# Tail scores of a cosine attention as two 64-row, 64-column products instead of one zero-padded full product, with a new order of the work

## The chip, the core and the metric

The kernel runs on one core of one Trainium2 chip. A core has a matrix engine (PE, whose weight loads are listed apart as PEld), a vector engine (DVE), an activation engine (ACT), a general engine (POOL) and a queue engine (SP), each with its own in-order list of instructions. The metric is the device time of one execution in microseconds (us); the median of several runs is compared.

## What is computed

Cosine attention over 8 batches, 12 heads, 448 tokens and a head size of 64, and then one highway layer over 3584 tokens of width 768:

```python
q_n = q / (np.linalg.norm(q, axis=-1, keepdims=True) + 1e-06)
k_n = k / (np.linalg.norm(k, axis=-1, keepdims=True) + 1e-06)
scores = np.matmul(q_n, k_n.transpose(0, 1, 3, 2)) / tau
attn = softmax(scores)                      # over the last axis
attn_out = np.matmul(attn, v)
x = attn_out.transpose(0, 2, 1, 3).reshape(B * S, H * D)
H = np.maximum(x @ w_h, 0.0)
T = 1.0 / (1.0 + np.exp(-(x @ w_t + b_t)))
out = T * H + (1.0 - T) * x
```

## The kernel before

The work is done batch by batch (`b`), and inside a batch by pairs of heads (`p`): head `p` and head `p + 6` share one tile of 128 partitions, 64 for each, because the head size is 64. For each batch the kernel squares and sums q and k (ACT and DVE), takes inverse roots by two Newton steps on DVE (L416 to L423, seven small instructions), scales q and k (`qn` L434, `kp` L495, `kb` L502, mostly on POOL), turns them with PE transposes (L446, L460, L465) and copies the results back with DVE (`qT` L451, `kT` L471 to L475).

The 448 keys of a head are three chunks of 128 and a tail of 64. `scores` (from L524) makes, for each pair of heads:

- for each of the three chunks two products of 64 rows by 128 columns (L531), one for each head. The one reads partitions 0 to 63 and the other 64 to 127, and each writes a PSUM tile `B` of its own;
- for the tails of both heads one product of 128 rows by 128 columns (L542). Columns 384 to 511 of `kT` come from `kb`, in which rows 0 to 63 are filled for the first head's columns alone and rows 64 to 127 for the second head's; the rest was set to zero at the start (L266). So one full product gives both heads' tail scores in one tile, 64 partitions each;
- an exponential on ACT for each of the seven tiles (L537 into `E`, L544 into `Et`).

`attend` (from L548) multiplies the exponentials with v: full products of 128 by 128 (L556 from `Et`, L561 from `E`) and, for the last 64 queries, products of 128 rows by 64 columns, two of which stand side by side in one tile (L569). DVE divides by the sums (L576, L577). The layer (`ffn`, from L583) turns x (L600), multiplies it with `wt` and `wh` (L616, or in two halves of 64 columns L613 for the last rows of a batch), and DVE, ACT and POOL make the gate and the output (L625 to L642), which SP stores (L649, L652).

So PE works with matmuls of three shapes: 128 by 128 (letter F in the code), 64 by 128 (letter T: L531) and 128 by 64 (letter C: L569 and L613). The letter is the `mode` given to each operation. Nothing that runs reads it: it belongs to the search that wrote the order.

All operations are listed first (1915 of them, from the loop at L656), and `ORDER` (L18) is a written-out permutation of them. It sets the order of instructions on every engine and of the loads and stores on every queue. `SLOTS` (L97) says which buffer of its ring each tile takes; `B` has eight PSUM buffers. Semaphores between engines follow from the order and the buffers. `PORT` adds a wait of some POOL operations on a DVE operation before them in the order.

At the start 18 products of zeros (L279) keep PE busy while the first q and k arrive.

Of the kernel before, what the change touches and what calls it, by code (L numbers as in the profile page):

```python
# [95 lines left out]

SLOTS = {  # L97
    "qr": "01010101",
    "kr": "0120120",
    "kt": "01010101",  # L100
    "kb": "01010101",
    "kp": "012345012345012345012345012345021435021435120534",
    "vr": "01010101",
    "vt": "01011010",
    "vp": "01010101",
    "sq": "0120120102102102102102012012022102102102102021020",
    "n2": "01010101",
    "y": "01201201",
# [661 lines left out]
```

## Time and profile before

| | |
|---|---|
| median of three runs | 271.36 us (271.6, 271.36, 269.6) |
| the profiled execution's own time | 270.06 us |
| its span from first to last instruction | 268.3 us |
| mean granted PE clock | 0.958 |
| PE busy | 251.6 us (94%), 3042 matmuls |
| DVE busy | 233.4 us (87%) |
| ACT busy | 214.5 us (80%) |
| POOL busy | 169.8 us (63%) |

A row of a group of instructions reads: line, engine, operation, tile written and tile read, shape (for a matmul rows\*columns of the array, then the moving operand), count, and then busy time in us, mean duration of one in ns, and the idle time just before them with what ended it. A row of the timeline starts with the start in us from the span's start and the duration of the merged instructions. A matmul's duration reaches to its modelled end, long after the next one has begun; what a matmul costs PE is the distance from its start to the next start.

### The profile page before, as it was taken

Reading aid. Unit: us, or ns where it says so; the run is one execution under the profiler, and the core shown is the slowest. Engines: PE = TensorE matmul, PEld = TensorE weight load, DVE = VectorE, ACT = ScalarE, POOL = GpSimd, SP = SyncE. Lnnn points to the kernel's source line nnn. Section 1 sums busy time; section 2 is a strip of 40 time slices with the busy share of each in tenths; the row PEclk is TensorE's granted clock in tenths of the full one; section 3 lists DMA queues with packets and bytes.
Section 4 is the critical chain, followed back from the end, with each engine's and each line's share of the span. In section 5 each row is a group of like instructions: output and inputs, shape, how many; then the busy total and the mean of one; then the engine's idle time right before and its main releaser. Section 6 shows DMA issues by size and latency. Waiting matters only on the chain.

```text
span 268.3 us, 7687 instructions
## 1 busy us (share of the span) xinstructions
PE 251.6 (94%) x3042; PEld 158.8 (59%) x3042; DVE 233.4 (87%) x523; ACT 214.5 (80%) x421; POOL 169.8 (63%) x212
## 2 busy tenths in 40 slices
PE   8375999999999999999999999999999999999990
PEld 2122566656756576657656685666666675667660
DVE  2987988799999999999989899999998788657993
ACT  3389899999589997999899996999979757883120
POOL 6467878306975679668957397659555686320650
PEclk9755799999999999999999999999999999999998
DMA  7999999999307990496995972990513101052146
GB/s 173 298 290 181 208 270 261 213 255 126 44 18 221 234 182 14 146 257 159 151 142 185 164 107 67 330 135 4 147 23 100 29 15 49 0 147 65 29 135 190
DMA packets 51092, 38.64 MB, mean 144 GB/s; under 512 B 37488, under 2 KB 47856, under 8 KB 51056
## 3 DMA queue, kind: packets, MB, share of 16 engines
q1 hardware_dynamic: 25888, 26.75, 36.2%
q0 software_dynamic: 24896, 11.21, 33.1%
q8 instruction: 24, 0.39, 0.5%
q10 hardware_dynamic: 272, 0.20, 0.2%
q14 instruction: 12, 0.10, 0.1%
HBM read 38.34 MB, written 11.01 MB: 184 GB/s over the span
## 4 chain that ended last, share of the span: by engine, by line
PE 81%; DMA 6%; DVE 4%; ACT 4%; SPq 1%; issue 1%; POOL 1%; ACTq 0%; DVEq 0%
PE B L616 33%; PE B L531 12%; PE B L561 10%; PE B L613 5%; DMA os<-in_k_dram 4%; PE B L556 4%; PE B L600 4%; PE B L446 3%; PE B L542 3%; PE B L569 3%; PE B L460 3%; ACT E L537 3%; DMA out_dram<-os 1%; PE B L465 1%; DVE hm L628 1%
## 5 line engine op out<-in xcount | busy, mean ns | idle before, releaser
L537 ACT ACTIVATE E<-B 128x448 f16<-128x448 f32 x288 | 137.4, 577 | 15.6 <-PE B L531 12.6
L642 POOL TENSOR_TENSOR os<-x,hm 128x384 f32<-128x384 f16 x53 | 47.5, 911 | 50.2 <-DVE hm L637 39.6
L616 PEld LDWEIGHTS <-xT 128*128 128x128 f16 x576 | 51.2, 98 | 34.8 <-issue 7.5
L434 POOL TENSOR_TENSOR qn<-qr,y 128x448 f16<-128x448 f32 x47 | 43.4, 934 | 24.6 <-issue 8.1
L616 PE MATMUL B<-wh,xT 128*128 128x384 f16 x288 | 57.6, 326 | 0.0
L616 PE MATMUL B<-wt,xT 128*128 128x384 f16 x288 | 56.7, 326 | 0.0
L531 PE MATMUL B<-qT,kT 64*128 64x448 f16 x288 | 43.5, 367 | 2.8 <-DVE kT L473 1.5
L561 PE MATMUL B<-vp,E 128*128 128x65 f16 x864 | 44.5, 195 | 0.0
L561 PEld LDWEIGHTS <-E 128*128 128x128 f16 x864 | 39.1, 99 | 2.9
L632 ACT ACTIVATE tt<-z 128x768 f16<-128x768 f32 (+1 forms) x32 | 25.3, 793 | 18.5 <-DVE z L625 14.8
L495 POOL TENSOR_TENSOR kp<-kr,y 128x384 f16<-128x384 f16 x42 | 34.3, 827 | 8.2 <-DVE tt L634 2.6
L628 DVE SCALAR_TENSOR_TENSOR hm<-B,x 128x384 f16<-128x384 f32 x56 | 30.5, 549 | 3.0 <-PE B L616 1.7
L556 PE MATMUL B<-vp,Et 128*128 128x130 f16 x144 | 32.3, 224 | 0.0
L625 DVE TENSOR_TENSOR z<-B,bias 128x384 f32<-128x384 f32 x48 | 25.9, 551 | 6.5 <-PE B L616 5.5
L544 ACT ACTIVATE Et<-B 128x448 f16<-128x448 f32 x48 | 27.9, 597 | 3.1 <-PE B L542 2.8
L577 DVE SCALAR_TENSOR_TENSOR x<-B,rd 128x448 f16<-128x448 f32 x48 | 29.2, 617 | 0.6
L376 DVE TENSOR_REDUCE n<-sq 128x14 f32<-128x896 f32 (+1 forms) x25 | 25.8, 1040 | 1.2 <-ACT sq L368 1.2
L397 DVE TENSOR_REDUCE n<-sq 128x18 f32<-128x1152 f32 (+2 forms) x17 | 21.5, 1269 | 4.2 <-ACT sq L388 3.8
L368 ACT ACTIVATE sq<-qr 128x896 f32<-128x896 f32 (+1 forms) x24 | 23.1, 978 | 1.1 <-DMA qr<-in_q_dram 1.1
L531 PEld LDWEIGHTS <-kT 64*128 64x128 f16 x288 | 10.3, 94 | 20.1 <-issue 12.3
L556 PEld LDWEIGHTS <-Et 128*128 128x128 f16 x144 | 14.1, 98 | 7.9 <-issue 4.7
L542 PE MATMUL B<-qT,kT 128*128 128x448 f16 x48 | 17.4, 371 | 1.1 <-DVE kT L475 1.1
(59 smaller groups left out, 363.3 us busy)
## 6 DMA issues: line engine op xcount, KB each, us to landing
qr<-in_q_dram SPq DMA_DIRECT2D x7, 1344.0 KB, 7.6
out_dram<-os SPq DMA_DIRECT2D x48, 192.0 KB, 3.3
kr<-in_k_dram POOLq DMA_DIRECT2D x7, 576.0 KB, 12.2
vr<-in_v_dram POOLq DMA_DIRECT2D x7, 576.0 KB, 10.3
kt<-in_k_dram SPq DMA_DIRECT2D x16, 96.0 KB, 6.4
vt<-in_v_dram SPq DMA_DIRECT2D x16, 96.0 KB, 7.5
out_dram<-os SPq DMA_DIRECT2D x16, 96.0 KB, 2.9
qr<-in_q_dram SPq DMA_DIRECT2D x3, 448.0 KB, 6.9
```

Of the source, the lines that this page charges most:

```text
L434: ENG[eng].tensor_mul(R("qn", 3 * b + g)[:, :, t, :], R("qr", b)[:, g + 3 * t, :].rearrange("l (j d) -> l j d", d=D), R("y", b)[:, c : c + ...
L495: ENG[eng].tensor_mul(R("kp", 6 * b + p).rearrange("l c t d -> l t c d"), a, kcol(b, p))
L531: nc.tensor.matmul(R("B", ("S", n, c, t))[:, 0:S], lhsT=R("kT", i)[ln, s, 128 * c : 128 * c + 128], rhs=R("qT", i)[ln, s, :], start=True, ...
L537: nc.scalar.activation(R("E", n)[:, at : at + 7, :].rearrange("l j x -> l (j x)"), R("B", ("S", n, c, t))[:, 0:S], AF.Exp)
L544: op("ACT", f"expt {n}", lambda: nc.scalar.activation(R("Et", n).rearrange("l j x -> l (j x)"), R("B", ("St", n))[:, 0:S], AF.Exp), r=[("B ...
L556: nc.tensor.matmul(U[:, 2 * c : 2 * c + 2, :], lhsT=Et[:, 2 * c : 2 * c + 2, :].rearrange("l j x -> l (j x)"), rhs=vp[:, 6:8, 0:65], start ...
L561: nc.tensor.matmul(U[:, 2 * c + t, :], lhsT=E[:, at : at + 2, :].rearrange("l j x -> l (j x)"), rhs=vp[:, 3 * t + m, 0:65], start=False, s ...
L577: op("DVE", f"ev {n}", lambda: nc.vector.scalar_tensor_tensor(out=R("x", b)[:, :, D * p : D * p + D], in0=U_()[:, :, 0:D], scalar=0.0, in1 ...
L616: nc.tensor.matmul(P[:, 0:MH], lhsT=xT[:, cc, :], rhs=w_[:, cc, MH * mh : MH * mh + MH], start=(cc == 0), stop=(cc == CC - 1))
L625: op("DVE", f"za {g} {mh}", lambda at=at, sl=sl: nc.vector.tensor_add(R("z", g)[:, sl], R("B", at)[:, 0:MH], biast[:, :] if tail else bias ...
L628: op("DVE", f"hm {g} {mh}", lambda at=at, sl=sl, mh=mh: nc.vector.scalar_tensor_tensor(out=R("hm", g)[:, sl], in0=R("B", at)[:, 0:MH], sca ...
L642: op(eng, f"out {g} {mh}", lambda sl=sl, mh=mh: ENG[eng].tensor_add(R("os", g)[:, sl], xpart(mh), R("hm", g)[:, sl]), r=[("gg", g), ("x", ...
```

## The change

The full tail product becomes two products of 64 rows by 64 columns. The first reads partitions 0 to 63 of `kT` and `qT` and writes partitions 0 to 63 of the tile; the second does the same with partitions 64 to 127. Both write the same PSUM tile. The exponential after them, the zeros in `kb` and the transposes stay. PE gets 48 matmuls and 48 weight loads more. The operation's letter goes from F to T. `ORDER` and `SLOTS` are replaced throughout, so every engine and every queue has a new order of the same operations. Lines after L543 move by three: the tail products are L544 and their exponential L547 in the changed kernel.

```diff
 ORDER = tuple(
     int(n)
     for n in """
-6 26 41 25 5 43 4 42 16 24 27 14 1 2 29 45 28 44 54 46 47 56 35 48 49 50 51 55 52 8 53 33 3 34 37 94 306 36 0 308 12
...
-1891 1897 1898 1906 1909 1900 1910 1907 1899 1672 1908 1911 1912 1913 1901 1914
+1 26 25 6 5 35 24 29 9 4 23 28 8 11 27 7 3 16 18 19 30 12 17 2 33 14 45 43 20 41 10 34 46 21 44 22 32 13 42 15 31 56
...
+1904 1897 1905 1898 1909 1906 1861 1910 1899 1907 1900 1908 1901 1911 1912 1913 1914
 """.split()
 )
...
-    "kp": "012345012345012345012345012345021435021435120534",
+    "kp": "012345012354012345012435012345012345130245130245",
...
         def ft():
-            nc.tensor.matmul(R("B", ("St", n))[:, 0:S], lhsT=R("kT", i)[:, s, 384:512], rhs=R("qT", i)[:, s, :], start=True, stop=True)
-        op("PE", f"qkt {n}", ft, r=[("qT", i, s), ("kT", i, "t")], w=[("B", ("St", n))], mode="F")
+            for t in range(2):
+                ln = slice(64 * t, 64 * t + 64)
+                nc.tensor.matmul(R("B", ("St", n))[ln, 0:S], lhsT=R("kT", i)[ln, s, 384 + 64 * t : 448 + 64 * t],
+                                 rhs=R("qT", i)[ln, s, :], start=True, stop=True)
+        op("PE", f"qkt {n}", ft, r=[("qT", i, s), ("kT", i, "t")], w=[("B", ("St", n))], mode="T")
```

What the new order moves can be read from the built programs. On PE, most of the 48 tail products stood between full products before; now 13 pairs stand inside a run of L531, and all others but one at an end of such a run. At the start, POOL issues the first two loads of v ahead of the zeroing of `vp` (before: between its two halves); SP issues the first tails of k after two more of the first loads of k, and the first tails of v after all first loads of q and k; DVE has both copies of the first values (L509) ahead of the last step of the first Newton iteration (before: the first of them ran at 19.5 us), and the first `kT` copy ahead of the second half of the first `qT` copy. The last 24 products of PE and everything after them stand as before, with other buffers.

More of the change, by code (lines that the diff above doesn't have):

```diff
@@ L101 @@
     "kb": "01010101",
-    "kp": "012345012345012345012345012345021435021435120534",
+    "kp": "012345012354012345012435012345012345130245130245",
     "vr": "01010101",
-    "vt": "01011010",
+    "vt": "01010101",
     "vp": "01010101",
-    "sq": "0120120102102102102102012012022102102102102021020",
+    "sq": "0120120120122102012012012102100120212011012021120",
     "n2": "01010101",
     "y": "01201201",
-    "tu": "010101010101",
-    "qn": "012012012012012012021021",
+    "tu": "010110101010",
@@ L111 @@
+    "qn": "012012012021021012012102",
     "qT": "012012012012012012012012",
     "kT": "012012012012012012012012",
-    "E": "012012012100210211021021021201201021021201210202",
-    "Et": "012010210122102011201201201121021211021021210210",
-    "rd": "010101010101010101010101010101010101010101010100",
+    "E": "012012012011210120210212021201201201201201102202",
+    "Et": "012012102100201020210210201201021021021021012012",
+    "rd": "010101010110101010100101011010101010101010101010",
     "x": "01201201",
-    "xT": "01220120120121021021021201200210",
@@ L118 @@
-    "z": "01011010100101010101010101011010",
-    "tt": "01100101011010010100101001001010",
-    "hm": "01201021201202102102012101020120",
-    "os": "01230120230210323012021302131230201",
-    "B": (
-        "0123456701234567012345670124761462074357410523714501204503216402564731206471035246357243170463514267"
-        "0352416105246310724625713604236175467137632576013425617305340621743074602510243715623015621435604605"
-        "3176453102645367524103675214074316425137542613026301426541275104304157350175240671425042034215047165"
-        "4027365412751620516243546273150423156027435067132740631647210635740625317023465023167402315401637542"
-        "6540216427031265473627051346203637512016745321734527014630612745312745613042631541257631405732461567"
-        "4302175235701645031756243501623741056423104276510623641725107456301725370316745302614753014672"
+    "xT": "01201201201202102102102012011201",
@@ new lines @@
+    "z": "01011011010101010101011010101010",
+    "tt": "01010101101010101010101001010101",
+    "hm": "01201012120102102102012201201021",
+    "os": "01230123012020130130310231023120321",
+    "B": (
+        "0123456701234567012345670124015672305167346230472046232561470234265710247132054670542630746135270512"
+        "7302641376525074630215734602173405252402302716405231674251765310742631053612746572103572315047560324"
+        "1057361542610356407123560742106754320175462037461256073075361743157602436571032754106210476513426734"
+        "1263514073604175306706254673267031245763410236541726543071043527614032576041567034215607135204312765"
+        "0364523670247160352473641053264051430214250361740126543702415067342640715635746302136231075431620576"
+        "1453021570312654215346721354201572634016532041573215604237152043157604361570231754236051273461"
```

142 rows, old and new, of the table ORDER are left out of this document.

## The prediction

> **What bounds the kernel now.** I read the page first: the busy shares, the slices, and the chain that ended last.
>
> ```profile
> span 268.3 us, 7687 instructions
> PE 251.6 (94%) x3042; PEld 158.8 (59%) x3042; DVE 233.4 (87%) x523; ACT 214.5 (80%) x421; POOL 169.8 (63%) x212
> ...
> PE   8375999999999999999999999999999999999990
> ...
> PEclk9755799999999999999999999999999999999998
> ...
> PE 81%; DMA 6%; DVE 4%; ACT 4%; SPq 1%; issue 1%; POOL 1%; ACTq 0%; DVEq 0%
> ```
>
> PE makes up 81% of the chain, and from the sixth slice on (about 34 us) it is full in every slice but the last. A full PE row alone proves little, because a matmul's end is modelled. So I took the groups of PE with their idle time in the first 35 us, and the busy time by stretch.
>
> ```profile
> L531 PE MATMUL B<-qT,kT 64*128 64x448 f16 x26 | 7.5, 497 | 2.7 <-DVE kT L473 1.5 <-DVE qT L451 0.7 <-ACT E L537 0.3
> L279 PE MATMUL B<-wz 128*128 128x512 f16 x18 | 6.8, 559 | 1.3 <-DVE wz L266 1.3
> ...
> L446 PE MATMUL B<-ident,qn 128*128 128x128 f16 x21 | 2.4, 280 | 4.1 <-DVE tu L421 4.1
> ...
> L542 PE MATMUL B<-qT,kT 128*128 128x448 f16 x4 | 2.0, 560 | 1.1 <-DVE kT L475 1.1
> L465 PE MATMUL B<-ident,kb 128*128 128x128 f16 x6 | 1.2, 298 | 1.0 <-DVE kT L473 1.0
> ```
>
> ```profile
> 34.40:262.00 227.60, 227.33 (x2878) 147.53 (x2875) 205.88 (x443) 191.00 (x377) 145.74 (x173) 1.00 0.63 130
> ```
>
> All that PE waited for others lies in the first 35 us (4.1 + 2.7 + 1.1 + 1.0, and 1.3 before the first product of zeros). Between 36 and 262 us the list of PE's waits is empty: of 227.60 us it is busy for 227.33. So from about 34 us to the end of the last product the time is the sum of PE's issue distances: a tenth of a microsecond more or less on PE is a tenth in the result, and there is no wait that could swallow it.
>
> **The change part by part: the products.** What a matmul costs PE is the distance of starts, which the timeline shows to 0.01 us.
>
> ```profile
> 101.19 0.50 PE L600 MATMUL B<-ident,x 128*128 128x128 f16 x6
> 101.52 0.55 PE L446 MATMUL B<-ident,qn 128*128 128x128 f16 x7
> ...
> 102.89 0.50 PE L600 MATMUL B<-ident,x 128*128 128x128 f16 x6
> 103.32 0.74 PE L531 MATMUL B<-qT,kT 64*128 64x448 f16 x6
> 103.99 1.15 PE L616 MATMUL B<-wt,xT 128*128 128x384 f16 x6
> 104.98 0.35 PE L542 MATMUL B<-qT,kT 128*128 128x448 f16 x1
> 105.17 1.14 PE L616 MATMUL B<-wt,xT 128*128 128x384 f16 x6
> 106.24 0.55 PE L531 MATMUL B<-qT,kT 64*128 64x448 f16 x4
> 106.72 0.51 PE L460 MATMUL B<-ident,kp 128*128 128x128 f16 x6
> ...
> 110.48 0.28 PE L569 MATMUL B<-vp,E 128*64 128x65 f16 x6
> 110.61 0.20 PE L569 MATMUL B<-vp,Et 128*64 128x65 f16 x2
> 110.73 0.23 PE L556 MATMUL B<-vp,Et 128*128 128x130 f16 x1
> ```
>
> The full tail product takes 0.19 us (104.98 to 105.17). Six L531 take 0.67 us and four take 0.48, so one pair of 64-row products costs 0.19 us too: the two run beside each other. A pair of 64 by 64 products that overlap in the same way streams the same 448 columns, so it costs 0.19 us as well. The zero rows of the full product never cost time; streaming gains nothing (48 x 0.00 us). The nearest weight load to the 48 new ones:
>
> ```profile
> L569 PEld LDWEIGHTS <-E 128*64 128x64 f16 x288 | 8.1, 111 | 6.7 <-issue 5.1 <-ACT E L537 0.5
> ```
>
> Uncovered they would cost 48 x 0.111 = 5.3 us. But the six L569 above, each with such a load, issue within 0.13 us: the loads hide under the products. I cost them at 0.
>
> **The switches between shapes.** The same rows show what it costs to change the shape. Six L616 take 0.99 us before a full product and 1.07 before an L531 (+0.08). Six transposes take 0.33 before full ones and 0.43 before an L531 (+0.10). Leaving L531 costs 0.67 - 3 x 0.19 = 0.10. For shapes that differ in columns alone I took another window.
>
> ```profile
> 98.63 0.35 PE L561 MATMUL B<-vp,E 128*128 128x65 f16 x6
> 98.81 0.22 PE L556 MATMUL B<-vp,Et 128*128 128x130 f16 x1
> 98.88 0.35 PE L561 MATMUL B<-vp,E 128*128 128x65 f16 x6
> 99.16 0.28 PE L569 MATMUL B<-vp,E 128*64 128x65 f16 x6
> 99.28 0.20 PE L569 MATMUL B<-vp,Et 128*64 128x65 f16 x2
> 99.31 0.98 PE L613 MATMUL B<-wh,xT 128*64 128x384 f16 x10
> ```
>
> Six L561 take 0.18 us before another full product and 0.28 before an L569 (+0.10); two L569 take 0.03 before an L613 of the same shape (99.28 to 99.31), and 0.12 before a full product (110.61 to 110.73, +0.09). So every change of shape costs (0.08 + 0.10 + 0.10 + 0.10 + 0.09) / 5 = 0.094 us, whether rows or columns differ; where the shape stays, as from L569 to L613, nothing is paid.
>
> I then walked PE's list of both built programs and counted changes of shape. Before there are 176. After there are 222 if 64 by 64 is a shape of its own: 55 of them are between a tail pair and an L531. There are 167 if it counts as the same as L531, as the letter T assumes. What a change between 64 by 128 and 64 by 64 costs, no row of before shows. The bounds are 0 us (as between L569 and L613) and 0.10 us. I take 0.094: the nearest row is 128 by 128 to 128 by 64, where rows are equal and columns differ as here, and it pays in full in both directions. That is 46 x 0.094 = +4.3 us. With 0 it is -9 x 0.094 = -0.85 us.
>
> The Trainium skill, page "TensorEngine Tiling (Array Packing)", section "Tiling Modes", lists 64x64 and 64x128 as two configurations and says that changing the mode, not just the tile, drains the engine. By that rule the sum stays +4.3 us, and the letter T would have been the wrong label; the trace agrees for the three shapes that it shows, and no row here has the fourth.
>
> **The start.** The new order also changes the first 34 us, in which PE waits for others. On DVE, two value copies now stand inside the first Newton iteration.
>
> ```profile
> 6.12 0.55 DVE L397 TENSOR_REDUCE n<-sq 128x6 f32<-128x384 f32 x1 [3.83 <-ACT sq L388]
> ...
> 9.92 0.18 DVE L423 SCALAR_TENSOR_TENSOR y<-tu,y 128x20 f32<-128x20 f32 x1
> 10.01 0.94 DVE L397 TENSOR_REDUCE n<-sq 128x12 f32<-128x768 f32 x1
> ...
> 11.34 0.62 DVE L434 TENSOR_TENSOR qn<-qr,y 128x448 f16<-128x448 f32 x1
> ...
> 14.42 0.35 DVE L473 COPY kT<-B 128x384 f16<-128x384 f16 x1
> ...
> 15.65 1.72 POOL L502 TENSOR_TENSOR kb<-kt,y 64x384 f16<-64x384 f32 x2
> ...
> 19.54 0.45 DVE L509 COPY vp<-vr 128x576 f16<-128x576 f16 x1
> ```
>
> ```profile
> vr<-in_v_dram POOLq DMA_DIRECT2D x2, 144.0 KB, 6.6
> ```
>
> The two copies (2 x 0.45) and the reduction (0.94), which comes forward too, would end the iteration 1.8 us later. Against that, the reductions of q no longer wait behind that of k (0.55 us), and the first `qn` of DVE, which ran at 11.34 us behind the 0.94 us reduction, does not have it ahead any more; the first transposes on PE need both halves, so they hardly move. The first `kT` copy, at 14.42 us the last thing before the first L531, comes forward by one `qT` half and one `kp`, 0.9 us in all. On SP the first tails of k now go behind two loads of k, and their square and sum come later too; `kb`, which needs the sum, ran only at 15.65 us on POOL, which covers that. So a gain of up to 0.9 us is one end. The other: the copies wait for the first loads of v, which land 6.6 us after issue; they are issued a microsecond or so earlier than before, at some 1.3 us, and land near 8 and 9 us, in time. If they take 2.5 us more, DVE and all behind it (`qn`, `kp`, the `qT` copy, then PE) are late by that: +2.5 us. I take 0, since the two named effects nearly cancel and the loads are near to in time.
>
> The steady order is new as well, on every queue. PE had no wait there and becomes slower, so DVE (205.88 of 227.60 us), ACT and POOL get more room: I cost it at 0, covered by PE; should one load or ring be late, its price is that wait. The loads and stores stay the same in number and size. The end (last gate, output, store) is the same sequence: 0.
>
> **The sum.** 268.3 + 4.3 + 0 = 272.6 us of span; the execution's own time is 270.06, 1.8 above its span, so 274.4. The median of the three runs, 271.36, is 1.3 us above this execution and one run (269.6) is below it. I set the forecast between: the mean of the four executions is 270.7, plus 4.3 gives 275.0 us.
>
> **Rivals.** First, on the other side: 64 by 64 is the same mode as 64 by 128 and no change is paid inside a run of L531. The sum is then -0.85 us: 269.8 us. It speaks for it that the row halves are the same; against it, that a change of columns alone is paid between L561 and L569. The point of decision: with 55 changes at x each, the total is -0.85 + 55x, so it is not slower from x below 0.015 us. Second, the two products do not overlap. Each pair then costs 2 x 0.19, and 48 x 0.19 = 9.1 us come on top: 284.1 us. For it speaks that the two L531 of a pair write two PSUM tiles, while these write one; against it, that the pairs of L569 write halves of one tile and overlap (two in 0.03 us). The same page's section "Restrictions and Gotchas" says that different row tiles cannot use one PSUM bank at a time, which would be this rival; no row here has two row halves in one bank. Third, the new start wins more than I see, by 2 to 3 us of the 8.9 that PE waits for q and k there: 272.5 us.
>
> **How the numbers follow.** Forecast 0.67, with its own range 273.2 to 277.6 us (start -0.9 to +2.5, and some for the spread of runs); no change paid 0.15; no overlap 0.08; a shorter start 0.10. A measurement of this kernel can tell about 1% from no change, here 268.6 to 274.1 us. Slower by over 1%: 0.58 of the forecast's 0.67, and 0.08, together 0.66. Within: 0.09 + 0.10 + 0.11 = 0.30. Faster: the rest of the first rival, with a shorter start, 0.04. The range from 269.4 to 277.6 us takes in the first and third rivals and leaves out the second and tails.
>
> **What would show it.** In the changed trace's timeline, the product before a tail pair inside a run of L531 shows 0.29 us to the next start, not 0.19, and again on the way back; a single pair takes 0.19 us plus that. If the way there and back costs nothing, the first rival holds; if the two starts of a pair are 0.19 us apart, the second. PE's waits should again end near 34 us; a later first row of L569, or waits on ACT, DVE or DMA after 40 us, would show that the new order, not the shape, moved the time. I am wrong above all if the fourth shape is not its own mode.

## The result, and the profile after

The changed kernel takes 273.12 us (median of 9 runs, 272.1 to 274.77). The kernel before took 269.74 us beside it (9 runs, 269.17 to 271.6). The ratio is 1.0112, with a 95% interval of 1.0081 to 1.0144: slower by 2.2 to 3.9 us, in the middle 3.0; the two medians lie 3.4 apart. The forecast was 275.0 us, from a base of 270.7 and a loss of 4.3. The direction held, and so did the range over the rivals, 269.4 to 277.6 us. The forecast's own range, 273.2 to 277.6, was missed by 0.1 us: the result lies just below it. Of the 1.9 us between forecast and median, 1.0 is the base (269.74 is the better measured one) and 0.9 is the loss itself.

These lines of the page after answer to those shown of before: span and busy times, PE's and the clock's slices, the chain by engine.

```profile
span 271.1 us, 7813 instructions
...
PE 254.8 (94%) x3090; PEld 157.6 (58%) x3090; DVE 231.7 (85%) x523; ACT 214.9 (79%) x421; POOL 170.1 (63%) x212
...
PE   8278899999999999999999999999999999999990
...
PEclk9757999999999999999999999999999999999998
...
PE 85%; DVE 6%; issue 3%; ACT 2%; DMA 1%; SPq 1%; POOL 1%; DVEq 0%
```

PE's fourth slice is fuller than before (8 for 5) and its clock there higher (7 for 5), and PE has more of the chain (85% for 81%); yet the span is 2.8 us longer, 271.1 for 268.3. The busy times by stretch (PE, PEld, DVE, ACT, POOL, then granted clock, DMA share, GB/s) show where nothing is lost:

```profile
0.00:34.40 34.40, 24.54 (x192) 12.01 (x193) 27.36 (x80) 25.54 (x48) 24.43 (x40) 0.80 1.17 242
34.40:265.00 230.60, 230.23 (x2900) 145.61 (x2898) 202.23 (x440) 189.25 (x374) 145.66 (x173) 1.00 0.63 126
```

From 34.4 us on PE is busy for 230.23 of 230.60 us, and the list of its waits is again empty from 36 us on. So the new time is not a wait. PE's waits of the whole execution (releaser, then us in total, times, longest) all lie in the start:

```profile
PE B L446 <- POOL qn L434: 5.2, 1, 5.2
PE B L279 <- DVE wz L266: 1.3, 1, 1.3
PE B L531 <- DVE kT L473: 1.2, 2, 0.8
PE B L559 <- ACT Et L547: 0.5, 1, 0.5
PE B L531 <- ACT Et L547: 0.5, 1, 0.5
```

With four more of 0.2 us they make 9.5 us, before about 10.0. The place that the prediction named is in the timeline of PE:

```profile
38.53 0.35 PE L564 MATMUL B<-vp,E 128*128 128x65 f16 x6
38.81 0.38 PE L544 MATMUL B<-qT,kT 64*64 64x448 f16 x2
39.12 0.36 PE L531 MATMUL B<-qT,kT 64*128 64x448 f16 x2
39.41 0.38 PE L544 MATMUL B<-qT,kT 64*64 64x448 f16 x2
39.72 0.36 PE L531 MATMUL B<-qT,kT 64*128 64x448 f16 x2
```

Read the distances of starts. Six L564 take 0.28 us before a tail pair (0.18 with no change behind them). The L531 pair between two tail pairs takes 0.29, where two such products take 0.19: the way into 64 by 64 costs 0.10. The tail pairs take 0.31: 0.12 more than the 0.19 of a full product with no change behind it. So 64 by 64 is a shape of its own, and both ways are paid.

### The profile page after: what moved, and what is told of

Read it like the earlier page. It is cut to its first block, busy times and chain, and to the rows that moved or that the text cites. A ratio compares the mean times of both kernels' runs of the same rounds, so it can differ in the third digit from the quotient of the medians.

```text
span 271.1 us, 7813 instructions
## 1 busy us (share of the span) xinstructions
PE 254.8 (94%) x3090; PEld 157.6 (58%) x3090; DVE 231.7 (85%) x523; ACT 214.9 (79%) x421; POOL 170.1 (63%) x212
## 4 chain that ended last, share of the span: by engine, by line
PE 85%; DVE 6%; issue 3%; ACT 2%; DMA 1%; SPq 1%; POOL 1%; DVEq 0%
PE B L619 35%; PE B L531 12%; PE B L564 9%; PE B L616 5%; PE B L544 5%; PE B L559 4%; PE B L603 4%; PE B L446 4%; PE B L572 3%; PE B L460 3%; DVE n L376 1%; PE B L465 1%; DMA kt<-in_k_dram 1%; ACT E L537 1%; DVE x L580 1%
## 5 line engine op out<-in xcount | busy, mean ns | idle before, releaser
L537 ACT ACTIVATE E<-B 128x448 f16<-128x448 f32 x288 | 137.9, 580 | 19.4 <-PE B L531 16.8
L619 PE MATMUL B<-wh,xT 128*128 128x384 f16 x288 | 55.6, 326 | 0.0
L619 PE MATMUL B<-wt,xT 128*128 128x384 f16 x288 | 54.9, 326 | 0.0
L531 PE MATMUL B<-qT,kT 64*128 64x448 f16 x288 | 43.9, 363 | 2.2 <-DVE kT L473 1.2
L564 PE MATMUL B<-vp,E 128*128 128x65 f16 x864 | 43.8, 195 | 0.0
L564 PEld LDWEIGHTS <-E 128*128 128x128 f16 x864 | 39.0, 99 | 1.9
L635 ACT ACTIVATE tt<-z 128x768 f16<-128x768 f32 (+1 forms) x32 | 25.1, 788 | 18.2 <-DVE z L628 12.4
L547 ACT ACTIVATE Et<-B 128x448 f16<-128x448 f32 x48 | 26.7, 579 | 3.0 <-PE B L544 3.0
L531 PEld LDWEIGHTS <-kT 64*128 64x128 f16 x288 | 10.8, 94 | 21.3 <-issue 14.4
L579 DVE RECIPROCAL rd<-B 128x7 f32<-128x7 f32 x48 | 9.5, 199 | 12.3 <-PE B L564 5.2
L605 DVE COPY xT<-B 128x768 f16<-128x768 f16 (+1 forms) x32 | 15.6, 499 | 4.1 <-PE B L603 3.8
```

The lines of the kernel that those rows point to most:

```text
L531: nc.tensor.matmul(R("B", ("S", n, c, t))[:, 0:S], lhsT=R("kT", i)[ln, s, 128 * c : 128 * c + 128], rhs=R("qT", i)[ln, s, :], start=True, ...
L537: nc.scalar.activation(R("E", n)[:, at : at + 7, :].rearrange("l j x -> l (j x)"), R("B", ("S", n, c, t))[:, 0:S], AF.Exp)
L547: op("ACT", f"expt {n}", lambda: nc.scalar.activation(R("Et", n).rearrange("l j x -> l (j x)"), R("B", ("St", n))[:, 0:S], AF.Exp), r=[("B ...
L564: nc.tensor.matmul(U[:, 2 * c + t, :], lhsT=E[:, at : at + 2, :].rearrange("l j x -> l (j x)"), rhs=vp[:, 3 * t + m, 0:65], start=False, s ...
L619: nc.tensor.matmul(P[:, 0:MH], lhsT=xT[:, cc, :], rhs=w_[:, cc, MH * mh : MH * mh + MH], start=(cc == 0), stop=(cc == CC - 1))
```

## The experiments

Three readings were to be told apart. The first is that of the prediction: each change of shape costs 0.094 us, and 64 by 64 is its own shape. The second is that the new order costs the time and the products do not. The third is that a pair of small products costs more in itself, wherever it stands. The counts of changes that follow are those of PE's list in each built kernel; before it is 176, in the changed kernel 222.

**The new order with the old product.** The changed kernel, with the full product of 128 by 128 put back:

```diff
-            for t in range(2):
-                ln = slice(64 * t, 64 * t + 64)
-                nc.tensor.matmul(R("B", ("St", n))[ln, 0:S], lhsT=R("kT", i)[ln, s, 384 + 64 * t : 448 + 64 * t],
-                                 rhs=R("qT", i)[ln, s, :], start=True, stop=True)
+            nc.tensor.matmul(R("B", ("St", n))[:, 0:S], lhsT=R("kT", i)[:, s, 384:512], rhs=R("qT", i)[:, s, :], start=True, stop=True)
```

> The new order with the old full 128 by 128 tail product (the order alone). Theory A (64 by 64 is a shape of its own; each change to or from it costs 0.094 us, and leaving it 0.024 us more; the new order has a start that is 1.6 us shorter): PE's list has 197 changes of shape instead of 222 and no leaving of the fourth shape, so 25 x 0.094 + 43 x 0.024 = 3.4 us less than the changed kernel: about 269.7 us, ratio to before 1.000, and PE's lead at the start stays. Theory B (the new order is slower by itself, whatever the shape): stays at 273.1 us, ratio 1.012. Theory C (each added product costs PE some 0.07 us by itself): 48 x 0.07 = 3.4 us less, 269.7 us; this run does not tell A from C.

Measured: 271.08 us (12 runs) beside 270.4 (23 runs), ratio 1.0024, interval 1.0 to 1.0049. The order alone costs at most half a per cent, so the second reading falls; the products account for the other 0.9% or so (1.0112 against 1.0024), some 2.4 us, where the expectation had 3.4. By the first reading the products are 222 - 197 = 25 changes, 2.4 us without the dearer way out.

The two kernels have the same order, so the same operation can be found in both traces, and the difference of its start times holds all that PE lost up to there. First the first transposes of q of the second batch, then the last twelve products, in the changed kernel:

```profile
36.76 0.56 PE L446 MATMUL B<-ident,qn 128*128 128x128 f16 x7
...
263.58 1.14 PE L616 MATMUL B<-wh,xT 128*64 128x384 f16 x12
```

and in this one:

```profile
36.39 0.56 PE L446 MATMUL B<-ident,qn 128*128 128x128 f16 x7
...
261.06 1.14 PE L613 MATMUL B<-wh,xT 128*64 128x384 f16 x12
```

Between the two places the changed kernel loses 2.52 - 0.37 = 2.15 us, and it has 20 changes more there: 0.107 us for each. The same place as above in this kernel's timeline:

```profile
38.35 0.35 PE L542 MATMUL B<-qT,kT 128*128 128x448 f16 x1
38.63 0.36 PE L531 MATMUL B<-qT,kT 64*128 64x448 f16 x2
38.93 0.36 PE L542 MATMUL B<-qT,kT 128*128 128x448 f16 x1
39.22 0.36 PE L531 MATMUL B<-qT,kT 64*128 64x448 f16 x2
```

A full product inside a run of L531 is two changes as well, 0.28 us to the L531 and 0.30 back. In such a place the split saves no change and loses none. Its way out is 0.31 for 0.28, its way in 0.29 for 0.30; in the trace's finer times such a tail costs 0.01 us more in all (twelve places from 36 us on). Most of the 25 changes come from tails that stand at the end of a run, next to full products, where the full product needed no change on that side.

**The old order with the new products.** The kernel before, with the edit of the products alone (the lines of the diff above, the other way round). 254 changes:

> The old order with two 64 by 64 products (the shape alone). In the old order nearly every tail product stands between full products, so PE's list has 254 changes of shape instead of 176. Theory A: 78 x 0.094 + 46 x 0.024 = +8.4 us over before, 278.1 us, ratio 1.031. Theory B (the order makes the time): no change, 269.7 us, ratio 1.000. Theory C (a price for each added product): +3.4 us, 273.1 us, ratio 1.012.

Measured: 277.96 us (6 runs), ratio 1.0274, interval 1.0239 to 1.031: +7.4 us, where the expectation had 8.4. The third reading would have given the 3.0 to 3.4 of the changed kernel again, since the pairs are the same 48. It falls. 254 - 176 = 78 changes at 0.094 make 7.3. Start by start, too: between the first transposes of the second batch (38.66 us, before 37.72) and the last twelve products (269.52, before 260.93) this kernel loses 7.65 us with 74 changes more, 0.103 for each. A tail between full products in this kernel:

```profile
106.96 1.15 PE L619 MATMUL B<-wt,xT 128*128 128x384 f16 x6
108.03 0.38 PE L544 MATMUL B<-qT,kT 64*64 64x448 f16 x2
108.34 1.15 PE L619 MATMUL B<-wt,xT 128*128 128x384 f16 x6
```

Six products of the layer take 1.07 us before the pair where before they took 0.99, and the pair takes 0.31 where the full product took 0.19: together 0.20 us for each tail that stood between full products.

**One product in the shape of L531.** The changed kernel, with one product of 64 by 128 in place of the pair. It leaves out the tail scores of the second head of each pair. 167 changes:

```diff
-            for t in range(2):
-                ln = slice(64 * t, 64 * t + 64)
-                nc.tensor.matmul(R("B", ("St", n))[ln, 0:S], lhsT=R("kT", i)[ln, s, 384 + 64 * t : 448 + 64 * t],
-                                 rhs=R("qT", i)[ln, s, :], start=True, stop=True)
+            nc.tensor.matmul(R("B", ("St", n))[:, 0:S], lhsT=R("kT", i)[0:64, s, 384:512],
+                             rhs=R("qT", i)[0:64, s, :], start=True, stop=True)
```

> The new order with one tail product of 64 rows by 128 columns, the shape of the other score products; it leaves out the tail scores of the second head of each pair. Here the letter T of the order is true: 167 changes of shape, none to a fourth one. Theory A: 55 x 0.094 + 43 x 0.024 = 6.2 us less than the changed kernel, 266.9 us, ratio to before 0.990; in the timeline one tail product inside a run of L531 takes 0.19 us and the way there and back costs nothing. Theory B: 273.1 us. Theory C (a price for each added product, and 48 fewer here): 269.7 us, ratio 1.000.

Measured: 268.91 us (12 runs), ratio 0.9944, interval 0.9914 to 0.9974. That is 1.7% below the changed kernel, some 4.5 us where 6.2 were expected. The timeline has the place that the expectation named:

```profile
40.20 0.71 PE L531 MATMUL B<-qT,kT 64*128 64x448 f16 x3
40.58 0.35 PE L542 MATMUL B<-qT,kT 64*128 64x448 f16 x1
40.77 0.35 PE L531 MATMUL B<-qT,kT 64*128 64x448 f16 x1
41.05 0.28 PE L570 MATMUL B<-vp,E 128*64 128x65 f16 x6
```

From L542 to L531 it is 0.19 us: no change, nothing paid. What was missing lies in the start. At the first transposes of the second batch this kernel is 1.45 us behind the changed one (38.21 us for 36.76), at the last twelve products 3.79 ahead (259.79 for 263.58): between them it wins 5.2 us with 50 changes fewer, 0.105 for each. In the start the granted clock was halved a second time:

```profile
33.28 0.53 PE L562 MATMUL B<-vp,E 128*128 128x65 f16 x6
...
36.99 0.35 PE L562 MATMUL B<-vp,E 128*128 128x65 f16 x6
```

Six products with v are busy for 0.53 us at 33.28 and for 0.35 at 36.99, and the clock's slices of this kernel are at 0.5 in the third and fourth and, after a fifth at 0.9 or more, at 0.7 in the sixth.

**The halves in the other order.** Is it the half that comes last that makes the way out dearer?

```diff
-            for t in range(2):
+            for t in (1, 0):
```

> The changed kernel with the two 64 by 64 products of a tail in the other order (partitions 64 to 127 first). It asks what makes leaving the fourth shape dearer (0.305 us from the second product's start to the next start, against 0.282 us after L531). If the extra 0.024 us belongs to the product on the upper half as the last one, it goes, 1.0 us in the whole; if it belongs to the shape, the distance stays 0.305 us and the time stays at that of the changed kernel.

Measured in one run: 272.78 us, span 271.0. In its timeline the tail pairs take 0.30 and 0.31 us, starts being read to 0.01 us, as they do in the changed kernel:

```profile
39.32 0.38 PE L544 MATMUL B<-qT,kT 64*64 64x448 f16 x2
39.63 0.36 PE L531 MATMUL B<-qT,kT 64*128 64x448 f16 x2
```

In the trace's finer times the way out is 0.306 us in both. The extra 0.02 goes with the shape, not with a half. Whether it belongs to the change or to the pair itself is less clear: where two tail pairs follow each other and no shape changes between them (five places in the changed kernel), their starts lie 0.21 us apart, and two full products in those places lie 0.19 to 0.21 apart.

**The full product, moved out of the runs.** If a change costs 0.094, then the new order with the full product, and 19 of its tails moved by one or two places in PE's list to where no change is needed (165 changes for 197), should win 3.0 us:

```diff
-... 114 117 314 167 145 115 173 121 ...
+... 114 117 314 173 167 145 115 121 ...
```

(173 is a tail product; 18 more are moved like it. The lists of the other engines are the same as with the full product in the new order. Lines stand seven lower in this kernel and, apart from those with more zeros, in all that follow from it: the tail product is L535, the chunks' L524, the transposes of q L439.)

> The new order with the full tail product, and 19 of the 48 tail products moved by one or two places in PE's list (their exponentials behind them where needed), so that none stands inside a run of L531 any more: 165 changes of shape instead of 197. Theory A (changes of shape make the difference): 32 x 0.094 = 3.0 us less than the new order with the full product, about 267.4 to 268.1 us, ratio to before 0.991. Theory B (the steady order is what costs): no change from that kernel, ratio 1.002.

Measured: 271.38 us (12 runs) beside 269.95 (29 runs), ratio 1.0022, interval 0.9992 to 1.0052. The expectation missed: nothing was won. The two profiled executions say where the 3 us went. At the first transposes of the second batch this kernel is 2.1 us behind the one with the same lists and no moves (38.53 us for 36.39); 0.6 of that was there at the very first transposes (13.35 for 12.71), ahead of any moved product. From there to the last twelve products (261.88 for 261.06) it wins 1.3 us with 30 changes fewer, where 2.8 were due. PE's waits and its timeline show what is behind both:

```profile
PE B L535 <- DVE kT L468: 0.7, 1, 0.7
```

```profile
74.03 0.36 PE L524 MATMUL B<-qT,kT 64*128 64x448 f16 x2
74.33 1.15 PE L609 MATMUL B<-wt,xT 128*128 128x384 f16 x6
...
95.75 0.63 PE L524 MATMUL B<-qT,kT 64*128 64x448 f16 x2
96.31 0.36 PE L535 MATMUL B<-qT,kT 128*128 128x448 f16 x1
```

```profile
95.36 0.62 DVE L570 SCALAR_TENSOR_TENSOR x<-B,rd 128x448 f16<-128x448 f32 x1
```

One of the moved products (L535, the third pair's) now comes ahead of work that was ready, and waits 0.7 us for its copy: a wait that is not in the list of the changed kernel. And an L531 pair that takes 0.30 us with its change at 74.03 takes 0.56 at 95.75: the second of the two starts 0.29 us after the first, at 96.03 us. Such a late start is no row in the list of waits, it lies inside the merged row's busy time. It waits for its PSUM buffer: the tile that had the buffer before it, by `SLOTS`, is read last by the division on DVE (L570), which ends at 95.98. From the second batch's first transposes on there are nine such late pairs, 1.2 us in all, against five with 0.5 us in the kernel without the moves. In each of the nine the late product starts 0.05 us after the last reader of its buffer's former tile has ended, five times one on DVE and four times an exponential on ACT. That is half of the 1.5 us that were missing; the other half stays open.

**Zeros to hold the clock.** Run by run, the time went with the mean granted clock: the kernel above took 269.07 us at 0.978 and 272.31 at 0.941. A theory of that point was that the low clock at the start makes the difference between the kernels, and that more zero products would hold it up:

```diff
-        op("PE", f"wm {i}", lambda i=i: nc.tensor.matmul(R("B", ("W", i))[:, :], lhsT=wz[:, 0:128], rhs=wz[:, 128:640],
-                                                         start=True, stop=True), r=[("wz",)], w=[("B", ("W", i)), ("wm",)], mode="F")
+        def zeros(i=i):
+            for _ in range(2):
+                nc.tensor.matmul(R("B", ("W", i))[:, :], lhsT=wz[:, 0:128], rhs=wz[:, 128:640], start=True, stop=True)
+        op("PE", f"wm {i}", zeros, r=[("wz",)], w=[("B", ("W", i)), ("wm",)], mode="F")
```

In the kernel above:

> The same as full_moved with 36 products of zeros at the start instead of 18. They end near 12 us, before the first real product. Theory D (the granted clock is at half from some 10 us until PE has been dense for a while, and the length of that stretch is what differs at the start): the half-clock stretch begins later, the transposes and products between 13 and 17 us run in about half the time, and 0.5 to 1.5 us go: ratio to before 0.986 to 0.989. Theory E (the waits for q and k make the start, not the clock): no change from full_moved, 0.991.

In the kernel before:

> The kernel before with 36 products of zeros at the start instead of 18, nothing else. Theory D (clock): the half-clock stretch from 10.2 to 30.6 us begins at 13.6 us or later, and 0.5 to 1.5 us go: ratio 0.995 to 0.998. Theory E (waits): 1.000.

Measured: 270.41 us, ratio 1.0003 (0.9976 to 1.0029) for the first, and 270.76 us, ratio 1.0017 (0.999 to 1.0044) for the second. The stretch of half clock began later (at 15.5 and 14.3 us; 10.2 in the kernel before) and lasted to 32.6 and 27.9 us. In the old order it was shorter as well, 13.6 us for 20.4 in the profiled executions. Nothing is won that these runs can tell: the zeros put the stretch off and do not take it away, and a shorter stretch did not show in the median.

**The one bad move undone.** As the kernel with 19 moved tails, but the third pair's product stays where it was (18 moves, 167 changes):

```diff
-... 114 117 314 173 167 145 115 121 ...
+... 114 117 314 167 145 115 173 121 ...
```

> As full_moved, but the one tail product that was moved within the first 27 us (that of the third pair of heads) stands where the new order had it; the other 18 moves stay (167 changes of shape). Theory F (that one move made PE wait for the copy of the tail keys, 0.7 us in the trace, and lost the rest by the half clock that followed; after 50 us the moves gain 1.2 us net, since the second product of some pairs now waits for its PSUM buffer): 1.2 to 2 us less than full_moved, ratio to before 0.995 to 0.998. Theory G (the start of full_moved was only bad luck with the clock): no change, 1.002. Theory A without any loss: 0.991.

Measured: 269.53 us (12 runs) beside 270.54 (24 runs), ratio 0.9968, interval 0.9939 to 0.9997: by the two ratios half a per cent, some 1.5 us, below the kernel with that move, for one product; the two were measured on different chips, and their intervals overlap by a little (0.9992 to 0.9997). The wait of 0.7 us is gone from its list. In the profiled executions it is 1.1 us ahead at the second batch's first transposes (37.44 us for 38.53) and stays so, and 0.4 of that was there at the very first transposes, ahead of the moved product: 0.7 us, the length of the wait, is what the move can have cost there.

**The first scaling of q moved forward.** In the changed kernel DVE stands at the first sum of a k tail, behind which DVE's half of the first `qn` is queued. Timeline of the changed kernel:

```profile
10.06 0.52 ACT L402 ACTIVATE sq<-kt 128x384 f32<-128x384 f32 x1 [2.86 <-DMA kt<-in_k_dram]
...
10.62 0.55 DVE L404 TENSOR_REDUCE n<-sq 128x6 f32<-128x384 f32 x1 [0.45 <-ACT sq L402]
11.09 0.61 DVE L434 TENSOR_TENSOR qn<-qr,y 128x448 f16<-128x448 f32 x1
...
11.62 0.17 DVE L416 TENSOR_SCALAR y<-n 128x18 int32<-128x18 int32 x1
...
11.94 1.33 POOL L434 TENSOR_TENSOR qn<-qr,y 128x448 f16<-128x448 f32 x1 [6.23 <-issue]
...
13.33 0.93 PE L446 MATMUL B<-ident,qn 128*128 128x128 f16 x7 [5.23 <-POOL qn L434]
```

The chain is: the load of `kt`, its square on ACT, its sum on DVE, DVE's half of `qn`, the first step of the next Newton iteration (L416), POOL's half, the transposes. POOL's half needs nothing that DVE's makes; it is behind L416 in the order, and `PORT` makes it wait for that. This kernel does two things: it takes the k tail out of the chain, and it puts POOL's half ahead of DVE's, so that L416 no longer holds it (55 is the sum that waits for the tail, 93 and 94 are DVE's and POOL's halves of `qn`):

```diff
-... 53 55 93 309 58 65 94 67 ...
+... 53 94 93 55 309 58 65 67 ...
```

> As moved_late, and on DVE the sum over the first tails of k goes behind the first qn, and POOL's first qn ahead of DVE's in the order, so that neither waits for the first tails of k. Theory H (the wait for the tails of k is what made the first transposes of the changed kernel 1.2 us late, 13.33 us against 12.11): the first transposes start near 12 us; 0.5 to 1.0 us less than moved_late in the whole if the start hangs on them, ratio 0.992 to 0.995. Theory I (later work on DVE and ACT sets the start, and the transposes have slack): they come earlier, and the time stays at that of moved_late.

Measured: 268.59 us (10 runs), ratio 0.9935, interval 0.9908 to 0.9962; 0.9 us below the kernel without the move on the same chip, with intervals that still touch. Its timeline:

```profile
10.06 0.62 DVE L427 TENSOR_TENSOR qn<-qr,y 128x448 f16<-128x448 f32 x1
10.17 1.31 POOL L427 TENSOR_TENSOR qn<-qr,y 128x448 f16<-128x448 f32 x1 [4.45 <-issue]
...
11.54 0.93 PE L439 MATMUL B<-ident,qn 128*128 128x128 f16 x7 [4.68 <-DVE y L409]
```

Both halves run at once and the transposes start at 11.54 us, for 13.33 in the changed kernel and 12.94 in the kernel without this move. In the changed kernel DVE's half starts 0.9 us after the roots are ready (10.17 us) and POOL's 0.85 after that, so both things weigh about the same; no run has one without the other. Of the 1.4 us at the first transposes, 0.3 are left at those of the second batch (37.10 us for 37.44) in the two profiled executions, of which the later kernel's is the slowest of its ten runs.

**The same with the zeros.** The edit of the zeros on top of it:

> As moved_late_qn with 36 products of zeros at the start. In full_moved they gave 0.2 per cent, in the old order nothing. If the half-clock stretch costs time at the start, 0.3 to 1 us less than moved_late_qn; if not, the same time.

Measured: 268.49 us (9 runs), ratio 0.9928, interval 0.9902 to 0.9953: no difference to the kernel without the zeros. So the versions that beat both kernels, by 0.3 to 0.7%, keep the full product, take the new order, put the tails where PE's shape does not change, and have no moved product that waits at the start.

## Why the prediction was right, step by step

**PE bounds, nothing swallows.** Right. No wait of PE after 36 us, and the lost time is in issue distances, as the starts of the same operations in two kernels of one order show: 2.15 us for 20 changes, 7.65 for 74, 5.2 for 50.

**The products and their loads at 0.** Right. The 96 products of L544 are busy for 17.6 us in all, the 48 full ones for 16.8: two for one, in nearly the same time. The group in the changed kernel, and in the new order with the full product:

```profile
L544 PE MATMUL B<-qT,kT 64*64 64x448 f16 x96 | 17.6, 379 | 0.0
```

```profile
L542 PE MATMUL B<-qT,kT 128*128 128x448 f16 x48 | 16.8, 367 | 0.0
```

The two starts of a pair are 2 to 4 ns apart in the trace. The rival without overlap falls. By the rule of the Trainium skill, page "TensorEngine Tiling (Array Packing)", section "Restrictions and Gotchas", that row tiles cannot use one PSUM bank at a time, it would have held; here both halves write one PSUM tile, in different partitions, and at most 0.02 us of the 0.19 is lost.

**46 changes at 0.094.** Right, and the rival that no change is paid falls: 0.10 in and 0.12 out, where it needed less than 0.015. The Trainium skill, page "TensorEngine Tiling (Array Packing)", section "Tiling Modes", which lists 64x64 and 64x128 as two configurations, agrees. One size was off: the price from the nearest rows was right for the way in, but the way out of 64 by 64 takes 0.305 us for a pair, not 0.19 + 0.094. For 43 ways out that is 0.9 us, if it came on top in full. It does not: inside a run of L531 the full product pays 0.59 us for both ways as well, and not 2 x (0.19 + 0.094) = 0.57. The whole stretches above exceed 0.094 for each change by 0.3 to 0.7 us (2.15 for 1.9, 7.65 for 7.0, 5.2 for 4.7); I take +0.5.

**The start at 0.** The size was wrong, below its lower bound, and so was one reason. I weighted each matmul with its full-speed distance and took start minus the work ahead of it: at the place with 14 us of work done, PE is 25.1 us behind before and 23.5 after. The new start is 1.6 us shorter there, and 1.8 at the end of the list; I take 1.7. The bound was 0.9; the third rival, a start shorter by 2 to 3 us, came nearer than the forecast's 0. Yet the step "they hardly move" failed: the first transposes start at 13.33 us, before at 12.11 (12.71 with the full product and the same lists, so 0.6 to 1.2 us later). The first inverse roots are ready as before, at 10.17 us for 10.10, and DVE's half of the first `qn` starts a little sooner, at 11.09 us for 11.34. The reason that `kb` "ran only at 15.65 us on POOL, which covers that" looked at the k tail's user and not at DVE's queue, in which this half stands behind the waiting sum; with the sum behind it, it starts at 10.06. What made the transposes later than before is POOL's half, of which the prediction says only that the transposes need it. In the kernel before it ran ahead of DVE's:

```profile
10.24 0.94 POOL L434 TENSOR_TENSOR qn<-qr,y 128x448 f16<-128x448 f32 x1 [4.82 <-issue]
...
12.11 0.91 PE L446 MATMUL B<-ident,qn 128*128 128x128 f16 x7 [4.09 <-DVE tu L421]
```

In the new order it stands behind DVE's half and the L416 for which it waits, and it starts at 11.94 us and takes 1.33. What won more than this lost comes later: PE's first product with v, before and after:

```profile
28.06 0.29 PE L556 MATMUL B<-vp,Et 128*128 128x130 f16 x1
```

```profile
21.46 0.29 PE L559 MATMUL B<-vp,Et 128*128 128x130 f16 x1 [0.48 <-ACT Et L547]
```

PE gets work from the values 6.6 us sooner, where before it waited for q and k. And its clock is back sooner. The same stretch of both executions (before first; the third column from the end is the granted clock):

```profile
24.00:31.00 7.00, 6.21 (x56) 3.49 (x54) 5.71 (x11) 5.86 (x13) 6.83 (x10) 0.53 1.37 192
```

```profile
24.00:31.00 7.00, 6.09 (x68) 3.15 (x66) 6.97 (x20) 7.00 (x13) 6.48 (x8) 1.00 1.25 205
```

PE starts 68 matmuls for 56 in these 7 us. That the earlier work brought the clock back is argued and not shown: the runs with more zeros moved the stretch of low clock, in the old order shortened it, and won nothing.

**The sum.** 4.3 + 0.5 - 1.7 = +3.1 us; the ratio gives +3.0 (2.2 to 3.9), and the two profiled spans +2.8. For the new order with the full product the same terms give 21 x 0.094 - 1.7 = +0.3; its span is 0.3 longer. The forecast was near in part by luck: its base was 1.0 too high and it put a start that won 1.7 us at nothing, which together carry the result below its own range; the +0.5 that it also left out took a part of that back.

**What stays open.** Why the new start wins 1.7 us although its first transposes come later: the earlier values and the earlier clock are seen together, and no run separates them. And why fewer changes did not come back one for one with 19 tails moved: late partners that wait for a PSUM buffer are half of what was missing from the second batch on.

## What to carry to other kernels

Where PE is full, count the changes of matmul shape in its list and price each with a distance of starts from the timeline; a tile cut to fit, with rows and columns of its own, buys no streaming time if the moving operand stays as long, and adds changes. Put products of one shape beside each other before cutting them, but move them only past work that isn't waiting. When an instruction moves on an in-order queue, ask first what stands behind it there, and what it has to wait for in its new place, and only then who uses what it makes.

## What the runs showed that was not expected

The way out of 64 by 64 is the dearest here: 0.306 us from the pair's second start, whichever half is last, against 0.28 after an L531 pair and 0.285 to 0.296 after a full tail product. Two row halves that write different partitions of one PSUM tile start 2 to 4 ns apart, so they run beside each other. A pair of products can lose up to 0.29 us without any row in the list of waits, when the second one's PSUM buffer is still being read. The mean granted clock differs from run to run of one kernel (0.941 to 0.978), and its time by 1.2% (272.31 to 269.07 us), as much as the loss that was to be explained. That the clock makes this difference is not shown. In medians, the split and the order could only be told apart by several runs of each.
